# Long convolution with routed experts: three batches' experts move into the last selection, and the column loop gets more buffers

## The chip, the cores and the metric

The kernel runs on one core of one Trainium2 chip. The metric is device time in microseconds (us), the median of three runs. A core has five engines that run their own queues in order: TensorE (PE, with its weight loads shown as PEld), VectorE (DVE), ScalarE (ACT), GpSimd (POOL) and SyncE (SP), whose queue issues the plain DMAs.

## The reference

Four batches of 12608 rows with 128 channels. First a long convolution along the rows, by a Fourier transform, then a layer of experts on the 128 rows of each batch with the highest scores:

```
u = x * v
y = irfft(rfft(u, 2 * S) * rfft(h_filt, 2 * S))[:S]
x = x * y
scores = einsum('bsd,d->bs', x, w_gate)
out = x.copy()
for b in range(B):
    top_idx = argpartition(-scores[b], 128)[:128]
    xe = x[b, top_idx]
    ye = maximum(xe @ w1, 0) @ w2          # 128 -> 1024 -> 128
    out[b, top_idx] = xe + sigmoid(scores[b, top_idx])[:, None] * ye
```

`h_filt` is a small network of `pos_emb`, times a window, the same for all batches. All of it is float32.

## The kernel before

**Spectrum and tiles.** The filter's spectrum is made first (`h_hid`, `h_spec`) and kept in DRAM. Then the batches' channels go through the transform in tiles of four channels, 32 tiles a batch, 128 in all. A tile `t` passes: `stage_u` on GpSimd (two products, L215 and L216), `f_s1` on TensorE with two copies on ACT (L226, L227, L235), `dft` on TensorE (L243, copied at L246), `f_v`, `f_u`, `f_m`, `f_y` on DVE, `f_sd` on GpSimd (L420, L421; the very last tile's on DVE), and three tiles later `f_i` on TensorE, copied into `big` by ACT (L429).

**Column loop.** When a batch's 32 tiles are in `big`, `P1.run` makes the last stage, 116 columns in 29 steps of four (`hbs`), two steps to a block of eight (`blocks`, 15 of them, the last with one step). A step's matmuls (`mm`) take four matmuls for a plain column (L475) and two for a column whose sum and difference GpSimd made ahead (`comb`, L458, read at L470). `comb` makes up to four columns of each block from the third on; in batches 0 and 3 every second block gets three. `comb` has two buffers (`cm`), and is called at the end of each odd step for the block after the next. DVE multiplies a step's result with x (`fin`, L483), and `weigh` multiplies it with the gate's weights (L502), from which ACT sums each column's score (L504). The last two steps' scores are summed on DVE alone (L489). The blocks of x lie in four buffers (`xa`). Four blocks are loaded ahead, in the last tiles of the batch (`LA`). A block that is done is stored (L495), and then the load (L447) of a later block into the buffer of the block before it is issued; it waits for that store. Both stand in SP's queue.

**Selection and experts.** After the loop, the batch's 128 rows are found by a search for a threshold over the scores in 16 rounds (`TopK`, and `TopKS` with ACT doing the counts). A round counts on DVE or ACT (`counts`), adds over partitions on TensorE (`total`), and steps on DVE (`step`). Then `select` marks and numbers the rows (its last product on GpSimd is L756), `place` makes their indices (matmuls by `tots`, then L768, L772, L783), and `moe` gathers the rows (L792), loads the experts' weights (L795, L797), and computes: transpose, two halves of the first layer (L815), gate, second layer, sum (L825), scatter (L827).

**What orders it.** The selection of batches 0 to 2 runs as `Background`, a generator that is cut at `yield` marks. The tile loop calls `hook` with a letter at fixed places, and if the generator stands at that letter, its next piece is issued there: `p` behind the DFT on TensorE, `n` next to it (at least a tile after the last piece), `d` and `e` among DVE's work, `w` for GpSimd's indirect DMA, `s`, `t`, `x` for the weights and what follows. The generator of batch b goes on into the column loop of batch b + 1, where `run` calls hooks at each step and drains what is left. The last batch's selection runs alone at the end. So the experts of batches 0 and 1 lie in the column loops of batches 1 and 2, those of batch 2 in the tiles just ahead of the last loop, and those of batch 3 at the end.

The buffers share one `arena`; `OFF` gives their places. In the loops, the weights of the experts lie on `qs`, `mt` and `yz`, which the tiles use.

Of the kernel before, what the change touches and what calls it, by code (L numbers as in the profile page):

```python
# [21 lines left out]
NJ = N2 // 2 + 1  # L22
# [20 lines left out]
NE = 3  # L43
LA = range(32 - 10, 32 - 2, 2)
# [9 lines left out]
ARENA = _o  # L54
POS0, HID0 = 0, PJ * N1
# [21 lines left out]
def _tables():  # L77
# [36 lines left out]
    tk[:, 294:294 + NJ] = np.where(_valid(), 0.0, NEG)  # L114
# [23 lines left out]
def hyena_moe(ctx, tc, xg, x2, pos, bw, ww, wg, mw1, mw2, fo, c1, gx, cf, ci, wm, tk, zr, out):  # L138
# [295 lines left out]
    class P1:  # L434
        def __init__(self, b):
            self.b = b
            self.sc = small([128, NJ], f"sc_{b}", tag="sc")
            self.xa, self.s4, self.cm = {}, {}, {}
            self.mul = None
            self.nc = [NC if b in (1, 2) or k % 2 else NC - 1 for k in range(len(blocks))]  # L440

        def load_a(self, k):
            if k < len(blocks):
                j0, j1 = blocks[k]
                self.xa[k] = buf("xa", k, [128, 8, D])
# [3 lines left out]
        def comb(self, k):  # L449
# [4 lines left out]
            n = min(self.nc[k], j1 - j0)  # L454
            cm = buf("cm", k, [128, 2, NC, D])
# [22 lines left out]
        def fin(self, h):  # L478
# [3 lines left out]
            js = slice(ja % 8, ja % 8 + n)  # L482
            nc.vector.tensor_tensor(out=xa[:, js], in0=self.s4.pop(h)[:, :n], in1=xa[:, js], op=ALU.mult)  # L483
            self.weigh()
            if h < len(hbs) - 2:
# [6 lines left out]
            if ja + n == blocks[blk][1]:  # L492
# [3 lines left out]
                if blk:  # L496
                    self.load_a(blk - 1 + NX)
# [58 lines left out]
    class TopK:  # L556
        def __init__(self, b, sc, ones, f, hi, ms):
            self.b, self.sc, self.ones, self.f, self.hi, self.ms = b, sc, ones, f, hi, ms
            self.n = sc.shape[1]
# [63 lines left out]
        def rounds(self):  # L623
            for r in range(16):
# [8 lines left out]
                self.total()  # L633
                yield "d"
# [49 lines left out]
    def select(b, k, n, tr, ones, rs, ws):  # L684
# [66 lines left out]
        if b + 1 < B:  # L751
# [4 lines left out]
            nc.gpsimd.tensor_tensor(out=oh, in0=oh, in1=ws[:, :128], op=ALU.mult)  # L756
        else:
# [203 lines left out]
```

## Time and profile before

| | us |
|---|---|
| median of three runs (lowest, highest) | 978.84 (978.0, 980.4) |
| the profiled execution | 975.58 |
| its span | 973.8 |
| TensorE busy in the span | 912.4 |
| DVE, ACT, GpSimd busy | 853.9, 607.9, 763.7 |
| HBM read, written (MB) | 146.67, 41.42 |

In the profile, a line of the timeline or of a group has the line of the kernel, the engine, the operation, `out<-in` by the program's names, and the shape. Behind a bar or in square brackets stands the idle time of the engine ahead of it and what ended it. The list of waits has, behind the colon, the sum, the number and the longest of the waits. A row of windows has the stretch and its length, then for each engine its busy time and number of instructions, then the granted clock of TensorE as a share of full speed, the busy share of the DMA engines, and GB/s. A float32 matmul is recorded as two instructions. "arena" is the common buffer, so most tiles have that name; the line tells them apart.

The tiles up to the first column loop take about 160 us (from 118.8 to 278.4), then a loop and 32 tiles alternate, and the last selection begins at about 932 us.

### The profile page before, as it was taken

Reading aid. Unit: us, or ns where it says so; the run is one execution under the profiler, and the core shown is the slowest. Engines: PE = TensorE matmul, PEld = TensorE weight load, DVE = VectorE, ACT = ScalarE, POOL = GpSimd, SP = SyncE. Lnnn points to the kernel's source line nnn. Section 1 sums busy time; section 2 is a strip of 40 time slices with the busy share of each in tenths; the row PEclk is TensorE's granted clock in tenths of the full one; section 3 lists DMA queues with packets and bytes.
Section 4 is the critical chain, followed back from the end, with each engine's and each line's share of the span. In section 5 each row is a group of like instructions: output and inputs, shape, how many; then the busy total and the mean of one; then the engine's idle time right before and its main releaser. Section 6 shows DMA issues by size and latency. Waiting matters only on the chain.

```text
span 973.8 us, 37920 instructions
## 1 busy us (share of the span) xinstructions
PE 912.4 (94%) x15566; PEld 836.0 (86%) x15566; DVE 853.9 (88%) x1598; ACT 607.9 (62%) x1953; POOL 763.7 (78%) x714
## 2 busy tenths in 40 slices
PE   8999999999999999998989999989989999989925
PEld 5777789999999999997889998979989999979914
DVE  7999999999987999998977999979879999976784
ACT  6656545555558887854577878645678877545820
POOL 5898779999997499998985899988965999955700
PEclk9999999999999999999999999999999999989966
DMA  8144588667868866667688666667687666653830
GB/s 241 67 171 188 194 248 210 183 185 210 240 171 284 256 181 186 196 192 207 181 288 255 181 196 194 185 183 221 211 275 217 181 187 195 188 151 99 301 123 6
DMA packets 64960, 190.54 MB, mean 196 GB/s; under 512 B 8853, under 2 KB 15876, under 8 KB 64772
## 3 DMA queue, kind: packets, MB, share of 16 engines
q1 hardware_dynamic: 64532, 187.59, 63.4%
q8 instruction: 123, 2.02, 0.9%
q0 software_dynamic: 256, 0.52, 0.2%
q14 instruction: 49, 0.40, 0.1%
HBM read 146.67 MB, written 41.42 MB: 193 GB/s over the span
## 4 chain that ended last, share of the span: by engine, by line
PE 73%; DMA 10%; POOL 6%; DVE 5%; issue 3%; ACT 1%; SPq 1%; POOLq 0%; DVEq 0%; ACTq 0%
PE c L243 18%; PE c L226 14%; PE a L226 12%; PE a L227 7%; PE c L227 6%; DMA out_dram<-arena 5%; DMA arena<-in_x_dram 4%; PE c L379 3%; PE a L359 3%; PE c L359 3%; PE a L475 2%; POOL arena L421 2%; POOL arena L420 2%; POOL arena L215 1%; DVE ms L595 1%
## 5 line engine op out<-in xcount | busy, mean ns | idle before, releaser
L226 PE MATMUL c<-ci_sb,arena 128*56 128x116 f32 x2048 | 225.6, 263 | 0.0
L227 PE MATMUL c<-ci_sb,arena 128*55 128x116 f32 x2048 | 225.6, 263 | 0.0
L226 PE MATMUL a<-c_sb,arena 111*58 111x111 f32 x2048 | 219.9, 261 | 0.0
L227 PE MATMUL a<-c_sb,arena 111*57 111x111 f32 x2048 | 219.7, 261 | 0.0
L243 PE MATMUL c<-arena,cf_sb 128*64 128x222 f32 x2048 | 217.4, 351 | 2.2 <-DVE arena L414 1.9
L226 PEld LDWEIGHTS c<-ci_sb,arena 128*56 128x56 f32 x2048 | 208.3, 131 | 0.1
L227 PEld LDWEIGHTS c<-ci_sb,arena 128*55 128x55 f32 x2048 | 208.2, 130 | 0.0
L226 PEld LDWEIGHTS a<-c_sb,arena 111*58 111x58 f32 x2048 | 201.9, 133 | 6.6 <-issue 0.3
L420 POOL TENSOR_TENSOR arena<-arena 128x444 f32<-128x444 f32 x127 | 133.8, 1054 | 88.4 <-DVE arena L414 60.2
L227 PEld LDWEIGHTS a<-c_sb,arena 111*57 111x57 f32 x2048 | 201.8, 132 | 1.2
L235 ACT COPY arena<-a 128x444 f32<-128x444 f32 x256 | 135.6, 530 | 77.8 <-PE a L227 77.4
L243 PEld LDWEIGHTS c<-arena,cf_sb 128*64 128x64 f32 x2048 | 152.7, 137 | 28.8 <-ACT arena L235 2.3
L429 ACT COPY big<-c 128x928 f32<-128x928 f32 x128 | 118.3, 924 | 75.6 <-PE c L227 75.6
L504 ACT ACTIVATE arena<-arena 128x128 f32<-128x128 f32 x432 | 128.2, 298 | 45.2 <-DVE arena L502 44.4
L215 POOL TENSOR_TENSOR arena<-arena 111x460 f32<-111x460 f32 x128 | 150.2, 1173 | 0.0
L458 POOL TENSOR_TENSOR arena<-big 128x512 f32<-128x512 f32 (+2 forms) x104 | 119.2, 1182 | 36.4 <-PE c L470 21.4
L216 POOL TENSOR_TENSOR arena<-arena,wm_sb 111x460 f32<-111x460 f32 x128 | 139.4, 1089 | 10.0
L407 DVE TENSOR_TENSOR arena<-c,arena 128x888 f32<-128x888 f32 x128 | 138.4, 1081 | 3.8
L408 DVE TENSOR_TENSOR c<-c,arena 128x888 f32<-128x888 f32 x128 | 138.3, 1080 | 0.0
L421 POOL TENSOR_TENSOR arena<-arena 128x444 f32<-128x444 f32 x127 | 134.7, 1061 | 0.0
L246 ACT COPY arena<-c 128x444 f32<-128x444 f32 x128 | 67.8, 530 | 60.6 <-PE c L243 57.2
L475 PE MATMUL a<-big,gx_sb 128*64 128x128 f32 x1536 | 100.6, 274 | 2.4 <-DVE arena L483 1.1
(188 smaller groups left out, 1654.9 us busy)
## 6 DMA issues: line engine op xcount, KB each, us to landing
arena<-hd SPq DMA_DIRECT2D x128, 444.0 KB
arena<-in_xg_dram SPq DMA_DIRECT2D x128, 402.5 KB
arena<-in_x_dram SPq DMA_DIRECT2D x112, 224.0 KB
out_dram<-arena SPq DMA_DIRECT2D x112, 224.0 KB
hd<-arena SPq DMA_DIRECT2D x32, 444.0 KB
arena<-in_moe_w_dram SPq DMA_DIRECT2D x8, 512.0 KB
arena<-in_pos_dram SPq DMA_DIRECT2D x14, 222.0 KB
arena<-in_x_dram SPq DMA_DIRECT2D x8, 112.0 KB
```

Of the source, the lines that this page charges most:

```text
L215: nc.gpsimd.tensor_tensor(out=u[:, 0], in0=u[:, 0], in1=u[:, 1], op=ALU.mult)
L216: nc.gpsimd.tensor_tensor(out=u[:, 1].rearrange("p (s j) -> p s j", s=4), in0=u[:, 0].rearrange("p (s j) -> p s j", s=4), in1=sg, op=ALU.mult)
L226: nc.tensor.matmul(o[:h], lhsT=lhsT[:, :h], rhs=rhs, **kw)
L227: nc.tensor.matmul(o[NQ:NQ + m - h], lhsT=lhsT[:, h:], rhs=rhs, **kw)
L235: nc.scalar.copy(out=te[:, e], in_=tps[e])
L243: nc.tensor.matmul(pq[w][e * NQ:(e + 1) * NQ, c], lhsT=cf_sb[:, 2 * w + e], rhs=te[:, e, c], start=True, stop=True)
L407: nc.vector.tensor_tensor(out=mt, in0=uv, in1=ht[:, 0].unsqueeze(1).to_broadcast([128, 2, HC]), op=ALU.mult)
L408: nc.vector.tensor_tensor(out=uv, in0=uv, in1=ht[:, 1].unsqueeze(1).to_broadcast([128, 2, HC]), op=ALU.mult)
L420: eng.tensor_tensor(out=nat(sd[:, 0]), in0=nat(yz[:, 0]), in1=rev(yz[:, 1]), op=ALU.add)
L421: eng.tensor_tensor(out=nat(sd[:, 1]), in0=rev(yz[:, 0]), in1=nat(yz[:, 1]), op=ALU.subtract)
L475: nc.tensor.matmul(ps[t * NQ:(t + 1) * NQ, k], lhsT=gx_sb[:, o:o + NQ], rhs=ay[:, :, e * NJ + j], start=e == 0, stop=e == 1)
L504: nc.scalar.activation(out=wx[:, k], in_=wx[:, k], func=AF.Copy, accum_out=self.sc[:, ja + k:ja + k + 1])
```

## The change

- The experts of batches 0 to 2 no longer run in the background. Their selections end with the gather of the rows into a tile of their own, and `run` is called only after the background is drained; the loop has no hooks for it any more.
- A class `Experts` takes the three picked batches. In the last column loop it adds their gate sums on DVE (steps 4, 8, 12) and loads the weights once (steps 22 and 25). When the last selection starts, it transposes the three batches' rows, and in the rounds, behind each `total`, it issues one piece: half of a first layer, or half of a second one, or (with the next batch's first piece) the sum and the scatter. The last batch's experts are computed at the end, as before (`one`), with the same weights.
- The column loop has two more buffers for x and a third one for the sums, all three on `qs`, `mt` and `yz`. The two extra blocks are loaded, and the first three blocks' sums issued, at the beginning of `run`. All blocks have four columns of sums.
- `select` has one more `yield "n"` behind its last product on GpSimd, for batches 0 to 2.
- The last but one step's scores go the way of the others, by DVE and ACT; the mask is applied with `min` in the place of `add`.

```diff
 NE = 3
+MW = 22
...
+CE = OFF["qs"][0]
+XE = [CE + 2 * NC * D + k * 8 * D for k in range(2)]
...
-    tk[:, 294:294 + NJ] = np.where(_valid(), 0.0, NEG)
+    tk[:, 294:294 + NJ] = np.where(_valid(), -NEG, NEG)
...
-            self.nc = [NC if b in (1, 2) or k % 2 else NC - 1 for k in range(len(blocks))]
...
         def load_a(self, k):
             if k < len(blocks):
                 j0, j1 = blocks[k]
-                self.xa[k] = buf("xa", k, [128, 8, D])
+                o = k % (NX + len(XE))
+                self.xa[k] = buf("xa", o, [128, 8, D]) if o < NX else view(arena, XE[o - NX], [128, 8, D])
...
-            n = min(self.nc[k], j1 - j0)
-            cm = buf("cm", k, [128, 2, NC, D])
+            n = min(NC, j1 - j0)
+            o = (k - CB[0]) % 3
+            cm = buf("cm", o, [128, 2, NC, D]) if o < 2 else view(arena, CE, [128, 2, NC, D])
...
-                if j // 8 in CB and CO <= j % 8 < CO + self.nc[j // 8]:
+                if j // 8 in CB and CO <= j % 8 < CO + NC:
...
+            if h == len(hbs) - 1:
+                self.weigh()
             nc.vector.tensor_tensor(out=xa[:, js], in0=self.s4.pop(h)[:, :n], in1=xa[:, js], op=ALU.mult)
-            self.weigh()
-            if h < len(hbs) - 2:
+            if h < len(hbs) - 1:
+                self.weigh()
                 self.mul = xa[:, js], buf("wx", h, [128, HB, D])[:, :n], ja, n
             else:
...
                 if blk:
-                    self.load_a(blk - 1 + NX)
+                    self.load_a(blk - 1 + NX + len(XE))
...
-        def run(self, bg):
+        def run(self, ex):
             self.wg = ps2(1, [128, D], f"wg_{self.b}")
             nc.scalar.copy(out=self.wg, in_=wgb)
+            for k in range(len(XE)):
+                self.load_a(NX + k)
+            for k in range(3):
+                self.comb(CB[0] + k)
             for h in range(len(hbs)):
-                bg.now = h
-                bg.hook("p", 3)
                 self.mm(h)
                 self.fin(h)
-                if h % 2:
-                    self.comb(h // 2 + 2)
-                bg.hook("w", 2)
-                if h > 1:
-                    bg.hook("s")
-                bg.hook("t", 5)
-                bg.hook("x", 3)
-                bg.hook("n", 1)
-                for _ in range(3):
-                    bg.hook("d")
-            nc.vector.tensor_tensor(out=self.sc, in0=self.sc, in1=negm, op=ALU.add)
-            bg.drain()
+                if h % 2 and h // 2 >= CB[0]:
+                    self.comb(h // 2 + 3)
+                if ex:
+                    ex.hook(h, self.wg)
+            nc.vector.tensor_tensor(out=self.sc, in0=self.sc, in1=negm, op=ALU.min)
             return self.sc
...
                 yield "p"
                 self.total()
+                if self.ex:
+                    self.ex.step()
                 yield "d"
                 self.step(r)
...
             nc.gpsimd.tensor_tensor(out=oh, in0=oh, in1=ws[:, :128], op=ALU.mult)
+            yield "n"
...
-        ix = small([128, 1], f"ix_{b}", I32, tag=f"ix{k0}")
+        ix = small([128, 1], f"ix_{b}", I32, tag=f"ix{b}")
...
-    def moe(b, ix, ws, mb, ks):
...
+    of = out.rearrange("b p j d -> (b p j) d")
+
+    def gather(b, ix, xe):
+        nc.gpsimd.indirect_dma_start(out=xe, out_offset=None, in_=of[:(b + 1) * 2 * PR * NJ],
                                      in_offset=bass.IndirectOffsetOnAxis(ap=ix, axis=0))
...
+    def scatter(b, ix, xo):
+        nc.gpsimd.indirect_dma_start(out=of[:(b + 1) * 2 * PR * NJ],
+                                     out_offset=bass.IndirectOffsetOnAxis(ap=ix, axis=0), in_=xo, in_offset=None)
...
+    class Experts:
+        def __init__(self, picked):
+            self.picked = picked
...
+            self.m1, self.m2 = view(arena, o, [128, 1024]), view(arena, o + 1024, [128, 8, D])
+            self.hs = [view(arena, o + 2048 + 1024 * k, [128, 8, CAP]) for k in range(2)]
+            o = OFF["te"][0]
+            self.xt = view(arena, o, [128, n, CAP])
+            self.tm, self.xo = (view(arena, o + n * CAP + k * D, [128, D]) for k in range(2))
+            self.gs = small([CAP, 2 * n], "gs", tag="gs")
+            self.gen = self.work()
+
+        def hook(self, h, wg):
+            if h % 4 == 0 and 0 < h // 4 <= len(self.picked):
+                self.gate(self.picked[h // 4 - 1][2], h // 4 - 1, wg)
+            if h == MW:
+                nc.sync.dma_start(self.m1, mw1)
+            if h == MW + 3:
+                nc.sync.dma_start(self.m2, mw2.rearrange("(c p) d -> p c d", p=128))
+
+        def gate(self, xe, k, wg):
+            nc.vector.scalar_tensor_tensor(out=self.tm, in0=xe, scalar=1.0, in1=wg, op0=ALU.mult, op1=ALU.mult,
+                                           accum_out=self.gs[:, 2 * k:2 * k + 1])
+
...
+        def half(self, xt, hs, ps, f):
...
+                cc = 4 * f + c
+                mm2(hp[:, c], self.m1[:, cc * 128:(cc + 1) * 128], xt)
+            nc.scalar.activation(out=hs[:, 4 * f:4 * f + 4], in_=hp, func=AF.Relu)
+
+        def second(self, yp, hs, c0, c1):
+            for c in range(c0, c1):
+                mm2(yp, hs[:, c], self.m2[:, c], start=(c == 0), stop=(c == 7))
+
+        def finish(self, b, ix, xe, yp, k):
+            nc.vector.scalar_tensor_tensor(out=self.xo, in0=yp, scalar=self.gs[:, 2 * k + 1:2 * k + 2], in1=xe, op0=ALU.mult,
+                                           op1=ALU.add)
+            scatter(b, ix, self.xo)
+
+        def start(self):
+            tp = ps1(2, [128, 512], "xeT")
+            for k, (b, ix, xe) in enumerate(self.picked):
+                nc.tensor.transpose(tp[:, k * CAP:(k + 1) * CAP], xe, ident)
+            nc.scalar.copy(out=self.xt, in_=tp[:, :len(self.picked) * CAP].rearrange("p (k c) -> p k c", c=CAP))
+            self.step()
+
+        def step(self):
+            next(self.gen, None)
+
+        def work(self):
+            last = None
+            for k, (b, ix, xe) in enumerate(self.picked):
+                hs = self.hs[k % 2]
+                self.half(self.xt[:, k], hs, 0, 0)
+                if last:
+                    self.finish(*last)
+                yield
+                self.half(self.xt[:, k], hs, 1, 1)
+                if k == 0:
+                    for i in range(len(self.picked)):
+                        self.sigmoid(i)
+                yield
+                yp = ps1(2, [128, 512], f"my_{b}")[:, :D]
+                self.second(yp, hs, 0, 4)
+                yield
+                self.second(yp, hs, 4, 8)
+                last = b, ix, xe, yp, k
+                yield
+            self.finish(*last)
+            yield
+
+        def one(self, b, ix, xe):
+            tp = ps1(0, [128, 512], f"xeTp_{b}")
+            nc.tensor.transpose(tp[:, :CAP], xe, ident)
+            xt = self.xt[:, 0]
+            nc.scalar.copy(out=xt, in_=tp[:, :CAP])
+            hs = self.hs[0]
+            for f in range(2):
+                self.half(xt, hs, f, f)
+            self.gate(xe, 0, wgb)
+            self.sigmoid(0)
+            yp = ps1(3, [128, 512], f"my_{b}")[:, :D]
+            self.second(yp, hs, 0, 8)
+            self.finish(b, ix, xe, yp, 0)
...
+    picked = []
+
+    def topk_one(b, sc, ex):
...
         k = (TopKS if b + 1 < B else TopK)(b, sc, onesb, f, hi, ms)
+        k.ex = ex
+        if ex:
+            ex.start()
         yield from k.rounds()
         yield "n"
...
-        yield from moe(b, ix, ws, mb, ((3, 3), (3, 3), (0, 1), (3, 2))[b])
+        xe = small([128, D], f"xe_{b}", tag=f"xe{b}") if b + 1 < B else ws[:, 128:256]
+        yield "w"
+        gather(b, ix, xe)
+        if ex:
+            warm(NWARM)
+            ex.one(b, ix, xe)
+        else:
+            picked.append((b, ix, xe))
...
-            if t >= NT - 3:
-                bg.hook("s")
-                bg.hook("t")
...
-            bg.hook("x")
...
-            bg.at = 0
-            sc = ph.pop(b).run(bg)
-            bg = Background(topk_one(b, sc))
+            bg.drain()
+            ex = Experts(picked) if b + 1 == B else None
+            sc = ph.pop(b).run(ex)
+            bg = Background(topk_one(b, sc, ex))
```

More of the change, by code (lines that the diff above doesn't have):

```diff
@@ L558, in __init__ @@
             self.b, self.sc, self.ones, self.f, self.hi, self.ms = b, sc, ones, f, hi, ms
+            self.ex = None
             self.n = sc.shape[1]
@@ L784, in place @@
         return ix
-    def moe(b, ix, ws, mb, ks):
-        xe, xt, tm = (ws[:, 128 * k:128 * k + 128] for k in range(3))
-        xo = ws[:, 384:512]
-        m1, m2, hs = mb
-        of = out.rearrange("b p j d -> (b p j) d")[:(b + 1) * 2 * PR * NJ]
-        yield "w"
-        nc.gpsimd.indirect_dma_start(out=xe, out_offset=None, in_=of,
-                                     in_offset=bass.IndirectOffsetOnAxis(ap=ix, axis=0))
-        yield "s"
-        nc.sync.dma_start(m1, mw1)
-        yield "t"
-        nc.sync.dma_start(m2, mw2.rearrange("(c p) d -> p c d", p=128))
-        yield "x"
-        if b + 1 == B:
-            warm(NWARM)
-        yield "p"
-        tp = ps1(ks[0], [128, 512], f"xeTp_{b}")
-        nc.tensor.transpose(tp[:, :CAP], xe, ident)
-        yield "d"
-        nc.scalar.copy(out=xt, in_=tp[:, :CAP])
-        gs = small([CAP, 2], f"gs_{b}", tag="gs")
-        wg = ps2(1, [128, D], f"wgm_{b}") if b + 2 < B else wgb
-        for hf in range(2):
-            yield "p"
-            hp = ps1(ks[hf], [128, 4, CAP], f"mh_{b}_{hf}")
-            for c in range(4):
-                cc = 4 * hf + c
-                mm2(hp[:, c], m1[:, cc * 128:(cc + 1) * 128], xt)
-            yield "d"
-            nc.scalar.activation(out=hs[:, 4 * hf:4 * hf + 4], in_=hp, func=AF.Relu)
-        yield "d"
-        nc.vector.scalar_tensor_tensor(out=tm, in0=xe, scalar=1.0, in1=wg, op0=ALU.mult, op1=ALU.mult,
-                                       accum_out=gs[:, 0:1])
-        nc.scalar.activation(out=gs[:, 1:2], in_=gs[:, 0:1], func=AF.Sigmoid)
-        yield "p"
-        yp = ps1(ks[0], [128, 512], f"my_{b}")
-        for c in range(8):
-            mm2(yp[:, :D], hs[:, c], m2[:, c], start=(c == 0), stop=(c == 7))
-        yield "d"
-        nc.vector.scalar_tensor_tensor(out=xo, in0=yp[:, :D], scalar=gs[:, 1:2], in1=xe, op0=ALU.mult, op1=ALU.add)
-        yield "w"
-        nc.gpsimd.indirect_dma_start(out=of, out_offset=bass.IndirectOffsetOnAxis(ap=ix, axis=0), in_=xo,
-                                     in_offset=None)
@@ L830, in topk_one @@
-    def topk_one(b, sc):
+    of = out.rearrange("b p j d -> (b p j) d")
+    def gather(b, ix, xe):
+        nc.gpsimd.indirect_dma_start(out=xe, out_offset=None, in_=of[:(b + 1) * 2 * PR * NJ],
+                                     in_offset=bass.IndirectOffsetOnAxis(ap=ix, axis=0))
+    def scatter(b, ix, xo):
+        nc.gpsimd.indirect_dma_start(out=of[:(b + 1) * 2 * PR * NJ],
+                                     out_offset=bass.IndirectOffsetOnAxis(ap=ix, axis=0), in_=xo, in_offset=None)
@@ L836, in topk_one @@
         ws = buf("ws", 0, [128, 640])
-        q0, u0 = OFF["qs"][0], OFF["u"][0]
-        mo = (u0 + 3 * 2 * XC, OFF["cm"][0], u0) if b + 2 == B else (q0, q0 + 1024, q0 + 2048)
-        mb = [view(arena, o, s) for o, s in zip(mo, ([128, 1024], [128, 8, D], [128, 8, CAP]))]
         rk, oh = yield from select(b, k, NJ, tri, onesb, rst, ws)
         ix = yield from place(b, rk, oh, jio, NJ, 3, ws[:, :128])
-        yield from moe(b, ix, ws, mb, ((3, 3), (3, 3), (0, 1), (3, 2))[b])
+        xe = small([128, D], f"xe_{b}", tag=f"xe{b}") if b + 1 < B else ws[:, 128:256]
[6 more added lines that the diff above has]
+            picked.append((b, ix, xe))
     for t in bank2[2:] + bank1 + bank2[:2]:
```

4 lines of the change are left out of this document (added).

## The prediction

> **What bounds the kernel now.** I read the page first, then the list of waits, then the chain of waits and the timeline around its irregular places, and last the windows.
>
> ```profile
> span 973.8 us, 37920 instructions
> PEclk9999999999999999999999999999999999989966
> PE 73%; DMA 10%; POOL 6%; DVE 5%; issue 3%; ACT 1%; SPq 1%; POOLq 0%; DVEq 0%; ACTq 0%
> ```
>
> The chain lies on TensorE for 73%, and the clock is full until the last two slices, the last selection. So three kinds of time can be won: TensorE work, holes in TensorE's queue, and the selection at the end. The list of waits names a hole and a transfer:
>
> ```profile
> PEld a L226 <- POOL arena L756: 10.4, 3, 3.5
> DVE arena L483 <- DMA arena<-in_x_dram: 21.1, 24, 2.5
> ```
>
> The first is three waits, one for each of the first three selections. The timeline shows what each costs, by the starts of the forward DFT (L243), one a tile:
>
> ```profile
> 455.28 0.54 PE L243 MATMUL c<-arena,cf_sb 128*64 128x222 f32 x4
> 459.89 0.54 PE L243 MATMUL c<-arena,cf_sb 128*64 128x222 f32 x4
> 442.48 0.41 PE L243 MATMUL c<-arena,cf_sb 128*64 128x222 f32 x2
> 446.76 0.46 POOL L756 TENSOR_TENSOR arena<-arena 128x128 f32<-128x128 f32 x1
> 450.67 0.54 PE L243 MATMUL c<-arena,cf_sb 128*64 128x222 f32 x4
> 646.06 0.41 PE L243 MATMUL c<-arena,cf_sb 128*64 128x222 f32 x2
> 655.90 0.54 PE L243 MATMUL c<-arena,cf_sb 128*64 128x222 f32 x4
> 851.65 0.41 PE L243 MATMUL c<-arena,cf_sb 128*64 128x222 f32 x2
> 862.75 0.35 PE L243 MATMUL c<-arena,cf_sb 128*64 128x222 f32 x2
> 857.00:860.00 3.00, 3.00 (x38) 3.00 (x36) 0.00 (x0) 0.53 (x1) 2.92 (x4) 0.50 0.00 0
> ```
>
> A plain tile takes 4.61 us (455.28 to 459.89). The tiles with the wait take 8.19, 9.84 and 11.10, and no later tile is shorter to make up for it. The last row is a window behind the third wait: its clock column reads 0.50, so that wait also left TensorE at half clock.
>
> **The change, part by part.** All of it against the profiled execution, 975.58 us for a span of 973.8.
>
> *The selection step.* `select` ends with a GpSimd product (L756) and `place` begins with matmuls that read it. They are issued at the head of the next tile, while GpSimd still has two products of `stage_u` ahead of L756; all of TensorE's tile queues behind them. The added step lets one tile pass. L756 ends at 447.22 (446.76 + 0.46); without the wait the next DFT starts at 442.48 + 4.61 = 447.09, and the matmuls follow that DFT, later than L756's end. So the waits go: (8.19 − 4.61) + (9.84 − 4.61) + (11.10 − 4.61) = 15.3 us. Next late is the gather, one tile later:
>
> ```profile
> 459.33 1.13 POOL L792 DMA_INDIRECT arena<-out_dram,ix  x1 [0.17 <-DVE arena L414]
> ```
>
> The first stands 17 us ahead of its loop (476.85, below), so a tile is covered. If that cover were gone, the drain ahead of the loop would pay, a tile at most (4.6).
>
> *The column loops.* Their first and last matmuls:
>
> ```profile
> 278.44 0.33 PE L475 MATMUL a<-big,gx_sb 128*64 128x128 f32 x2
> 322.77 0.61 PE L470 MATMUL a<-arena,gx_sb 128*64 128x128 f32 x8
> 476.85 3.71 PE L475 MATMUL a<-big,gx_sb 128*64 128x128 f32 x64
> 526.40 0.61 PE L470 MATMUL a<-arena,gx_sb 128*64 128x128 f32 x8
> 682.09 0.33 PE L475 MATMUL a<-big,gx_sb 128*64 128x128 f32 x2
> 732.00 0.61 PE L470 MATMUL a<-arena,gx_sb 128*64 128x128 f32 x8
> 884.54 0.33 PE L475 MATMUL a<-big,gx_sb 128*64 128x128 f32 x2 [1.03 <-ACT big L429]
> 927.23 0.61 PE L470 MATMUL a<-arena,gx_sb 128*64 128x128 f32 x8
> ```
>
> That is 44.9, 50.2, 50.5 and 43.3 us, together 188.9. The second and third carry an expert each:
>
> ```profile
> 504.28 0.32 PE L226 MATMUL c<-arena 128*64 128x128 f32 x1 [1.71 <-ACT arena L805]
> 510.26 0.32 PE L226 MATMUL c<-arena 128*64 128x128 f32 x1 [0.96 <-ACT arena L815]
> 515.87 0.32 PE L226 MATMUL c<-arena 128*64 128x128 f32 x1 [0.59 <-ACT arena L815]
> 517.67 0.39 PE L475 MATMUL a<-big,gx_sb 128*64 128x128 f32 x4
> ```
>
> Its second layer takes 1.8 us (515.87 to 517.67), the first has as many matmuls, the transpose is small: about 4 us of work and 3.3 of waits. Taking it out leaves 50.2 − 7.3 = 42.9. What TensorE alone needs comes from the steps:
>
> ```profile
> 486.78 0.33 PE L470 MATMUL a<-arena,gx_sb 128*64 128x128 f32 x2 [0.80 <-POOL arena L458]
> 520.29 0.28 PE L475 MATMUL a<-big,gx_sb 128*64 128x128 f32 x2
> ```
>
> From 517.67 to 520.29 are two steps: one with two summed columns takes 1.31 us. One of the four without takes 1.86 (64 matmul records, two steps, in 3.71): 4 × 1.86 + 25 × 1.31 = 40.2. GpSimd's first sums still come after its last tile, so the 0.8 above and a little before it stay, 1.2 as I estimate: 41.4. The first and last loop summed three columns instead of four in every second block; the change gives them the same 40.2, for a fourth column more of GpSimd time, which the third buffer and the earlier start cover.
>
> Now the transfers. A block is, by the code, 2 × 56 × 8 × 128 × 4 bytes in and as much out; two more buffers give two blocks of lead, but each load still waits for an output two places ahead of it in SP's queue.
>
> ```profile
> 483.21 1.06 POOL L421 TENSOR_TENSOR arena<-arena 128x444 f32<-128x444 f32 x1
> 485.25 0.79 SPq L495 DMA_DIRECT2D out_dram<-arena  x2
> 297.60 4.19 DMA out_dram<-arena
> 701.69 7.12 DMA out_dram<-arena
> 301.85 4.90 DMA arena<-in_x_dram
> 500.00:504.00 4.00, 2.48 (x42) 1.99 (x38) 2.48 (x4) 2.40 (x17) 3.59 (x4) 1.00 0.91 339
> ```
>
> The new buffers lie on `yz`, which GpSimd reads until 484.27, 7.4 us into the loop; the two new loads stand at SP's head until then, and the first outputs queue behind them. They leave at about 9, land at 14 and free the seventh block's load. From there two blocks take one output (4.2) and two issues of about 0.8, so 2.9 us a block; the 14th block lands at 14 + 7 × 2.9 + 4.9 = 39 us, about when TensorE is two steps from the end. So TensorE and transfers are nearly level. I take 42.5 for the first three loops (between 41.4 and 44.9, nearer the first as no load is waited for early), and 41.2 for the last, where GpSimd is free sooner and DVE has three gate sums to add. Sum 168.7, so −20.2 us.
>
> At 1.31 us a step the loop moves 918 KB in 2.62 us, 350 GB/s, above the 339 of the fullest window. The Trainium skill ("DMA: Bandwidth & Descriptors", Specifications) gives about 358 GB/s as the limit of one core's HBM traffic, by which the 41.4 could just be held; the window shows less.
>
> *The tiles ahead of the last loop.* There the third expert filled holes of TensorE. Without it the loop may start up to a microsecond earlier (the 1.03 in front of its first matmul), or 3.4 later if a hole of 3 us halves the clock as above. I take 0.
>
> *The last selection.* Sixteen rounds, with twelve pieces of 8 matmuls between them:
>
> ```profile
> 953.04 0.16 PE L226 MATMUL c<-st,onesb 128*64 128x3 bf16 x1 [1.16 <-DVE ms L595]
> 954.42 0.16 PE L226 MATMUL c<-st,onesb 128*64 128x3 bf16 x1 [1.16 <-DVE ms L595]
> 948.00:952.00 4.00, 0.65 (x6) 0.40 (x6) 3.41 (x27) 0.00 (x0) 0.00 (x0) 0.50 0.01 2
> L825 DVE SCALAR_TENSOR_TENSOR arena<-c,gs,arena 128x128 f32<-128x128 f32 x3 | 1.0, 346 | 4.4 <-PE c L227 4.4
> ```
>
> A round takes 1.38 us and leaves TensorE idle for 1.16. What waits behind a piece is the next round's total, on TensorE; behind an expert's result, the round's threshold, on DVE. A piece is half of a layer, 0.9 at full clock: hidden. At 0.50 it is 1.8, and each round grows by some 0.7. The row of 948 shows half clock, but with TensorE nearly idle; the pieces fill it. I take two slow rounds, 1.5, until the clock is up, and three results of 0.35 on DVE, partly inside its wait for TensorE: 0.7. Sum +2.2 (0.7 to 9.1). The three scatters run on an idle GpSimd, the weights load once, during the loop's last steps. The Trainium skill ("TensorE: Matmul & The Clock Gate", Part 1) has the clock go full after a busy window of about 3.4 us and half after an idle one; by that the slow rounds are two or three, as taken, and the rounds of the row of 948 agree with the idle half of it.
>
> The mask (`min` for `add`) and the reordered last weighing change no count on the path: 0.
>
> Sum: −15.3 − 20.2 + 0 + 2.2 = −33.3, so 942.3 us in a profiled execution. The median of the runs (978.84) is 3.3 above the profiled one, so 945.6.
>
> **The rivals.**
> 1. *The loops stay at the transfers' pace.* The first and last keep 44.9 and 43.3, the other two fall to 44.9: −10.9 instead of −20.2. For it: the 21.1 us of waits for inputs. Against: two blocks of lead. 954.9. Chance 0.13.
> 2. *The wait for L756 only moves* with its step, or the chain falls on another GpSimd result: 945.6 + 15.3 = 960.9. For it: GpSimd is busy 2.92 of 3 us in the row of 857. Against: the end at 447.22. This is also the case that the step does not do what it says. Chance 0.07.
> 3. *The pieces never lift the clock*: 12 × 0.7 = 8.4 instead of 1.5: 952.5. Chance 0.07.
> 4. *Slower: SP's queue chokes.* With both new loads at its head and more in flight, an output takes 7.1 us, as at 701.69, where weights shared the queue. A block then takes (7.1 + 1.6) / 2 = 4.35; a loop 14 + 8 × 4.35 + 4.9 + 1.3 = 55, the last some 51: 216, +27 for −20: 945.6 + 47 = 993. It beats the other gains once outputs take over about 6.2 us throughout (loops of 50.5). Against: the weights leave those loops. Chance 0.03.
>
> The forecast keeps 0.70. Faster by over 0.3% (about what a measurement here tells from no change) 0.95, within 0.02 (rivals 1 to 3 together with outputs of 6 us), slower 0.03.
>
> **Range.** Low: loops at 41.4 and 40.2 (−4.3), rounds at 0.7 (−1.5), −1 ahead of the last loop: 939. High: rival 1 with part of rival 3, and rival 3: 957. Rivals 2 and 4 lie outside, and about a tenth for sizes that are off.
>
> **What would show it.** No wait for L756 on TensorE, no tile over 6 us; loops of 41 to 43 us with waits for inputs under 2 us each; rounds of 1.4 us but for the first ones, clock 1.00 in the middle rounds. It is wrong if a GpSimd wait stands in the tile after, if L483 still waits 5 us or more a loop, or if the rounds stay near 2.1.

## The result and the profile after

The changed kernel takes 943.56 us (median of 6 runs, 941.11 to 948.21) against 978.66 for the kernel before in the same session (6 runs, 975.87 to 980.4): a ratio of 0.965, 95% interval 0.962 to 0.967. The forecast was 945.6 (939 to 957). The profiled execution took 944.23 us for a span of 942.3.

The head of the page, with the clock of the 40 slices and the chain of waits by engine:

```profile
span 942.3 us, 37826 instructions
PEclk9999999999999999999999999999999999999998
PE 79%; DVE 6%; POOL 5%; DMA 4%; ACT 3%; issue 3%; SPq 0%; POOLq 0%; ACTq 0%; DVEq 0%
```

The chain's share on TensorE rose from 73% to 79%, that of DMA fell from 10% to 4%: transfers were what gave way. The clock's digits now read 9, which stands for 90% or more, up to the last slice, through most of the rounds too.

The timeline around the step that follows the first selection (TensorE's forward DFT, now L246, once a tile, and the last GpSimd product, now L760):

```profile
442.33 1.72 PE L246 MATMUL c<-arena,cf_sb 128*64 128x222 f32 x16
446.97 1.70 PE L246 MATMUL c<-arena,cf_sb 128*64 128x222 f32 x16
451.81 0.54 PE L246 MATMUL c<-arena,cf_sb 128*64 128x222 f32 x3
446.64 0.46 POOL L760 TENSOR_TENSOR arena<-arena 128x128 f32<-128x128 f32 x1
```

The product ends at 447.10, the DFT starts at 446.97, and the matmuls that read the product come behind that DFT: as forecast to about a tenth of a microsecond. The tile takes 4.84 (446.97 to 451.81), where before there were 8.19, 9.84 and 11.10. The list of waits no longer has L760 ahead of TensorE.

The four column loops by windows (the stretch and its length; then busy time of PE, PEld, DVE, ACT, POOL with instructions; granted clock, DMA share, GB/s), and the wait of `fin` (now L489) for its inputs over the whole span:

```profile
279.20:322.50 43.30, 41.28 (x735) 40.03 (x734) 37.24 (x60) 31.98 (x201) 40.46 (x35) 1.00 0.71 232
473.40:516.90 43.50, 41.00 (x734) 40.06 (x734) 37.72 (x60) 32.05 (x201) 40.76 (x36) 1.00 0.72 233
667.40:709.40 42.00, 40.78 (x734) 40.07 (x734) 37.83 (x60) 32.31 (x202) 40.72 (x35) 1.00 0.71 237
854.60:894.60 40.00, 39.96 (x729) 39.80 (x730) 35.22 (x61) 32.95 (x208) 31.49 (x26) 1.00 0.71 230
```

```profile
DVE arena L489 <- DMA arena<-in_x_dram: 7.9, 10, 1.8
```

TensorE is busy for 39.96 of the 40.0 us of the last loop: there it is the bound. The waits for inputs fell from 21.1 us to 7.9 and lie, but for 0.3, in the first three loops (2.6, 3.0, 2.0).

Stage by stage, in microseconds of the profiled executions. A loop goes from its first matmul to the end of its last; "behind" is from there to the next loop's first matmul; the last selection goes from the last loop's end to the end of the span.

| kernel | loops | their sum | behind loops 1, 2, 3 | last selection | span |
|---|---|---|---|---|---|
| before | 44.9, 50.2, 50.5, 43.3 | 188.9 | 153.5, 155.1, 151.9 | 45.9 | 973.8 |
| after | 43.3, 43.5, 42.0, 40.0 | 168.8 | 150.9, 150.5, 145.2 | 47.7 | 942.3 |
| n_only | 44.1, 50.9, 50.2, 44.9 | 190.0 | 150.8, 151.1, 146.5 | 46.1 | 963.6 |
| no_n | 42.0, 42.3, 42.5, 40.0 | 166.7 | 155.3, 155.5, 151.5 | 46.6 | 954.3 |
| old_no_experts | 44.0, 44.6, 44.7, 44.6 | 178.0 | 155.5, 153.5, 151.3 | 46.3 | 964.7 |
| four_x | 45.9, 45.6, 44.8, 43.6 | 179.8 | 151.6, 150.6, 146.0 | 48.7 | 955.7 |
| late_loads | 42.0, 42.2, 42.0, 40.0 | 166.2 | 150.1, 150.1, 144.9 | 47.5 | 936.7 |

From before to after, the span fell by 31.5: loops −20.1, the three stretches −13.9, the last selection +1.8, and +0.8 ahead of the first tile, which the change does not touch.

### The profile page after: what moved, and what is told of

Read it like the earlier page. It is cut to its first block, busy times and chain, and to the rows that moved or that the text cites. A ratio compares the mean times of both kernels' runs of the same rounds, so it can differ in the third digit from the quotient of the medians.

```text
span 942.3 us, 37826 instructions
## 1 busy us (share of the span) xinstructions
PE 902.8 (96%) x15518; PEld 831.1 (88%) x15518; DVE 854.4 (91%) x1570; ACT 613.3 (65%) x1983; POOL 769.3 (82%) x714
## 4 chain that ended last, share of the span: by engine, by line
PE 79%; DVE 6%; POOL 5%; DMA 4%; ACT 3%; issue 3%; SPq 0%; POOLq 0%; ACTq 0%; DVEq 0%
PE c L246 18%; PE c L230 10%; PE c L229 10%; PE a L230 10%; PE a L229 9%; PE a L479 5%; PE c L382 3%; PE a L362 3%; PE c L362 3%; PE c L479 3%; PE a L474 2%; ACT arena L510 2%; DMA out_dram<-arena 1%; POOL arena L423 1%; POOL arena L424 1%
## 5 line engine op out<-in xcount | busy, mean ns | idle before, releaser
L229 PE MATMUL c<-ci_sb,arena 128*56 128x116 f32 x2048 | 224.8, 263 | 4.3 <-POOL arena L423 2.0
L246 PE MATMUL c<-arena,cf_sb 128*64 128x222 f32 x2048 | 217.6, 351 | 2.2 <-DVE arena L417 1.9
L229 PE MATMUL a<-c_sb,arena 111*58 111x111 f32 x2048 | 217.0, 259 | 0.0
L230 PE MATMUL a<-c_sb,arena 111*57 111x111 f32 x2048 | 216.8, 259 | 0.0
L229 PEld LDWEIGHTS c<-ci_sb,arena 128*56 128x56 f32 x2048 | 206.5, 130 | 5.9 <-POOL arena L423 2.2
L229 PEld LDWEIGHTS a<-c_sb,arena 111*58 111x58 f32 x2048 | 199.2, 132 | 4.3 <-issue 0.3
L230 PEld LDWEIGHTS a<-c_sb,arena 111*57 111x57 f32 x2048 | 199.0, 131 | 2.9
L246 PEld LDWEIGHTS c<-arena,cf_sb 128*64 128x64 f32 x2048 | 154.1, 137 | 27.6 <-ACT arena L238 2.3
L510 ACT ACTIVATE arena<-arena 128x128 f32<-128x128 f32 x448 | 133.0, 298 | 27.4 <-DVE arena L508 25.2
L462 POOL TENSOR_TENSOR arena<-big 128x512 f32<-128x512 f32 (+1 forms) x104 | 125.1, 1262 | 8.9 <-ACT big L432 5.6
```

The lines of the kernel that those rows point to most:

```text
L229: nc.tensor.matmul(o[:h], lhsT=lhsT[:, :h], rhs=rhs, **kw)
L230: nc.tensor.matmul(o[NQ:NQ + m - h], lhsT=lhsT[:, h:], rhs=rhs, **kw)
L246: nc.tensor.matmul(pq[w][e * NQ:(e + 1) * NQ, c], lhsT=cf_sb[:, 2 * w + e], rhs=te[:, e, c], start=True, stop=True)
L510: nc.scalar.activation(out=wx[:, k], in_=wx[:, k], func=AF.Copy, accum_out=self.sc[:, ja + k:ja + k + 1])
```

## The experiments

**n_only** and **no_n**: the later step alone, and everything but the step.

```
             nc.gpsimd.tensor_tensor(out=oh, in0=oh, in1=ws[:, :128], op=ALU.mult)
+            yield "n"        # n_only: added to the kernel before
-            yield "n"        # no_n: taken from the changed kernel
```

> The kernel before with the one added yield behind the last GpSimd product of select, and nothing else. Theory (the three TensorE waits for L756 are lost whole, and one tile is enough to hide them): the three long tiles of 8.2, 9.8 and 11.1 us fall to about 4.8, 14.6 us less: 964.0 from 978.7. Rival (the wait only moves to another GpSimd result or is paid in the drain): within 3 us of 978.7, and a tile over 7 us stays.

Measured: 965.27 (962.77 to 966.59), ratio 0.986 (0.982 to 0.991), against 976.14 for before then.

> The changed kernel without the added yield, all else kept. Theory (the step's gain does not hang on the other parts): three tiles of 8 to 11 us come back, +14.6: 958.2 from 943.6. Rival (with the experts gone from the background, GpSimd would be on time anyway): +5 at most.

Measured: 958.1 (955.4 to 962.44), ratio 0.981 (0.975 to 0.986). Without the step the wait is back on TensorE in the changed kernel:

```profile
PE a L229 <- POOL arena L760: 9.2, 3, 3.1
```

Its three tiles take 9.85 each instead of 4.84, +15.0 together, and its time is 14.5 above the changed kernel's. In n_only the three tiles fell by 14.6, but the span only by 10.2 and the time by 10.9: other stages of that one execution were longer by 4.4 (the loops alone by 1.1, the stretches less their tiles by 2.6; one later tile took 5.58). So the step takes about 15 us out of TensorE's tiles in either kernel. That no part of it comes back later is shown with the other parts of the change; for n_only, where the 4.4 come from stays open.

**old_no_experts**: the kernel before without the experts' layers of the first three batches (the rows are selected and gathered, nothing more; their weights are not loaded either), to see what the experts alone cost the loops.

```
-        yield from moe(b, ix, ws, mb, ((3, 3), (3, 3), (0, 1), (3, 2))[b])
+        if b + 1 < B:
+            yield "w"
+            nc.gpsimd.indirect_dma_start(out=ws[:, :128], ...)
+            return
+        yield from moe(b, ix, ws, mb, ((3, 3), (3, 3), (0, 1), (3, 2))[b])
```

> The kernel before with the experts of batches 0 to 2 left out (their rows are gathered and go no further, so out lacks their sums); buffers, sums and steps as before. Theory (the experts cost the loops their matmuls and their waits): the second and third loop fall from 50.2 and 50.5 to about 43, the last tiles by 0.8: 963.3 from 978.7, so -15.4. Rival (the transfers bind at the first loop's pace): both fall to 44.9 only, -11.6: 967.

Measured: 965.75 (963.46 to 966.49), ratio 0.986 (0.982 to 0.991). The second and third loop take 44.6 and 44.7, not 43, and the waits for inputs are as long as before:

```profile
DVE arena L483 <- DMA arena<-in_x_dram: 21.2, 29, 1.9
```

The rival was right: with four buffers, the loops fall only to the pace of the transfers.

**four_x**: the changed kernel without the two new input blocks.

```
-XE = [CE + 2 * NC * D + k * 8 * D for k in range(2)]
+XE = []
```

> The changed kernel with four input blocks instead of six (no extra loads at the head of run), three sums buffers and all else kept. Theory (two blocks of lead keep inputs ahead of TensorE): waits of L483's line for inputs rise from 8 to over 20 us, loops go to 44 to 45.5 us from 43.3, 43.5, 42.0 and 40.0: +6 to +10, 951.5. Rival (the experts' going alone made the loops short): +1 or less.

Measured: 956.26 (955.06 to 957.62), ratio 0.977 (0.973 to 0.981) against 0.965: some 12 us above the changed kernel. The waits are back:

```profile
DVE arena L489 <- DMA arena<-in_x_dram: 24.3, 23, 1.9
```

The four loops sum to 179.8 instead of 168.8. So the loops' 20.1 divide into 9.1 for all the rest (the experts above all) and 11.0 for the two blocks. Executions with six blocks scatter by some 2 us here: the sum is 166.7 in no_n and 169.2 in weights_early (below).

**two_sums**: the changed kernel with two sums buffers, as before.

```
-            o = (k - CB[0]) % 3
+            o = k % 2
...
-            for k in range(3):
+            for k in range(2):
...
-                    self.comb(h // 2 + 3)
+                    self.comb(h // 2 + 2)
```

> The changed kernel with two sums buffers instead of three and the sums issued two blocks ahead, all else kept. Theory (GpSimd at 2.5 us a block and TensorE at 2.62 are so close that two buffers lock them to each other): GpSimd waits for TensorE at each block, loops 0.5 to 1.5 us longer each: +2 to +5, 947. Rival (the third buffer does nothing, as GpSimd is never behind): within 1 us of 943.6.

Measured: 944.47 (942.09 to 946.65), ratio 0.965 (0.962 to 0.967), the loops at 167.3. The third sums buffer does nothing that can be measured.

**three_cols**: the changed kernel with the number of summed columns of before.

```
+            self.nc = [NC if b in (1, 2) or k % 2 else NC - 1 for k in range(len(blocks))]
...
-            n = min(NC, j1 - j0)
+            n = min(self.nc[k], j1 - j0)
...
-                if j // 8 in CB and CO <= j % 8 < CO + NC:
+                if j // 8 in CB and CO <= j % 8 < CO + self.nc[j // 8]:
```

> The changed kernel with the summed columns of before: three instead of four in every second block of the first and the last loop. My theory: a column that is not summed costs TensorE (1.86 - 1.31) / 2 = 0.28 us, six or seven of them 1.7 to 1.9; the last loop, at TensorE's pace, grows by that from 39.96, the first, which waits for inputs, by less than 1: +2, about 946. The rival, that both loops have slack: last loop 40.0 to 40.5, total as the changed kernel.

Measured: 943.28 (942.89 to 945.7), ratio 0.966 (0.963 to 0.968). The last loop takes 41.3 instead of 40.0, less than the 1.7 expected but the right direction; the first takes 42.8, no longer than in the changed kernel. In the whole time 1.3 us is not to be told from the scatter.

**no_pieces**: the changed kernel without the experts' layers of the first three batches (selected and gathered rows stay as they are).

```
-                if self.ex:
-                    self.ex.step()
...
-        if ex:
-            ex.start()
```

> The changed kernel with the experts of batches 0 to 2 left out (gathered, never computed nor scattered); weights and gate sums stay. Theory (in the rounds the pieces cost one cold piece ahead of the first total, 1.3 us, and the late second weight matrix, 1.5, and nothing else): rounds of 1.38 throughout, 2.8 us less: 940.8. Rival (pieces also cost each round through TensorE or DVE): 5 us less or more. Rival (the clock that the pieces keep up pays for them): the same 943.6.

Measured: 943.72 (941.83 to 944.82), ratio 0.965 (0.962 to 0.967). The last selection took 44.9 instead of 47.7, but other stages of this execution were longer, so the time shows nothing of it. The same code of the last selection took 45.4 to 49.7 in six executions (below), so three experts cost the rounds some 3 us and no more can be said; that the clock which the pieces hold up pays for them is not seen, since from the last step to the end both take about 18.1. In the kernel before, taking the experts out shortened the loops by 10.9 (188.9 to 178.0).

**weights_early** and **early**: where the last selection lost its 1.8. The first issues the experts' weights at steps 12 and 15 of the last loop instead of 22 and 25. The second also transposes the rows at step 20 and puts two pieces ahead of the rounds.

```
-MW = 22
+MW = 12
...
+            if h == MW + 8:          # early
+                self.turn()          # the transposes and their copy
...
+            self.step()              # early: a second piece ahead of the rounds
```

> The changed kernel with the weights issued at steps 12 and 15 of the last loop instead of 22 and 25. Theory (the 2.8 us round waits for the second matrix, which was issued at 897.8 behind outputs in SP's queue): that round falls to 1.4, 1.5 us less: 942.1. Rival (the weights then delay the loop's inputs): that round falls, but the last loop grows by as much: the same 943.6.

Measured: 946.13 (944.72 to 950.78), ratio 0.968 (0.966 to 0.971). The round of 2.8 us is gone, the longest take 1.81 and 1.79 at half clock; but the first step comes 8.5 us after the loop instead of 6.4, and why stays open.

> As weights_early, and the picked rows are transposed in the loop (step 20) and two pieces instead of one issued ahead of the first round. Theory (TensorE goes cold between the loop's end and the first piece, because the transposed rows are copied only behind ACT's last scores): pieces at full clock from the loop's end, the first total no later than DVE asks for it: 1.3 us less than weights_early, 940.8. Rival (the hole between the two pieces and the first total, about 2 to 3 us, makes it cold again): as weights_early, 942.1.

Measured: 945.77 (943.31 to 951.34), ratio 0.968 (0.965 to 0.970). In early all rounds without the search's half-way step take 1.35 to 1.39; the first steps (L617), from the timeline:

```profile
902.32 0.16 DVE L617 SCALAR_TENSOR_TENSOR st<-c,tk_sb 128x3 f32<-128x3 f32 x1
903.68 0.16 DVE L617 SCALAR_TENSOR_TENSOR st<-c,tk_sb 128x3 f32<-128x3 f32 x1 [0.15 <-PE c L230]
905.07 0.15 DVE L617 SCALAR_TENSOR_TENSOR st<-c,tk_sb 128x3 f32<-128x3 f32 x1
```

But the last loop then waits 2.1 us for its inputs (weights_early: 4.0) and takes 40.6 (40.1). Both were expected to be faster than the changed kernel, and neither time shows it.

**best**: both matrices, the transposes and their copy at step 20, right behind the last input load, and two pieces ahead of the rounds as in early.

```
-MW = 22
+MW = 20
...
-            if h == MW + 3:
                 nc.sync.dma_start(self.m2, mw2.rearrange("(c p) d -> p c d", p=128))
+                self.turn()
```

> The changed kernel with both weight matrices issued at step 20 of the last loop, right behind the last load of an input block, the rows of the three batches transposed there too, and two pieces of the experts ahead of the rounds. Theory: the late second matrix and the cold first piece were the 2.8 us by which the end of the last selection is longer than without pieces, and behind the last input load the weights delay no input: rounds all 1.36 to 1.39, last loop 40.0 to 40.3, no input wait over 1 us in it, total 941 to 942. The rival: the weights, ahead of the last outputs, hold back something else (the gather of the last selection, the first pieces), and the total is 943 to 946.

Measured: 942.36 (941.25 to 945.76), ratio 0.965 (0.962 to 0.968). The last selection took 45.0, with no input wait in the last loop, but that loop took 40.6, and the first round still took 1.88, at half clock. Kernels whose last selection has the code of the changed one show 45.4 (three_cols), 47.5 (late_loads) and 49.7 (two_sums), so neither 45.0 nor the time proves a gain.

**in_loop**: the pieces in steps 13 to 28 of the last loop instead of the rounds, the weights at steps 2 and 5. The pieces' results also go to other buffers in PSUM, the memory into which this kernel's matmuls write.

```
-MW = 22
+MW = 2
...
+            if h == 13:
+                self.start()
+            if h > 13:
+                self.step()
...
-                if self.ex:
-                    self.ex.step()
```

> The changed kernel with the twelve pieces of the first three batches' experts at steps 13 to 28 of the last column loop instead of the rounds of the last selection (weights loaded at steps 2 and 5). My theory, that time on TensorE in the last loop counts in full while in the rounds it is hidden: the loop ran at TensorE's pace (39.96 us), so it grows by 12 pieces of 0.93, about 11; the rounds go back to 1.38 each and the end of the selection gets 2.8 shorter: about +8, 951 to 953. The rival, that the loop has slack because transfers bind it: last loop +0 to +3, total 941 to 944.

Measured: 969.81 (968.21 to 975.01), ratio 0.993 (0.991 to 0.996). Neither expectation held: the last loop takes 66.2, 26.3 more. The list of waits inside it:

```profile
DVE arena L489 <- PE a L474: 15.0, 9, 2.6
POOL arena L462 <- PE a L474: 12.4, 3, 5.3
PE c L229 <- DVE arena L508: 8.7, 6, 1.5
PE c L229 <- ACT arena L850: 2.7, 1, 2.7
PE c L229 <- ACT arena L835: 2.0, 2, 1.0
```

TensorE's matmuls of the pieces (L229) waited 13.4 us: for the weighing (L508), for the copy of the transposed rows (L850) and for the relu (L835). All the matmuls of the next step stood behind them. With the work of 12 pieces of about 0.93 that is 25 of the 26. The 8.7 may come from where this kernel put the second layers' results, in the PSUM buffer of the gate weights that L508 reads; this was not told apart. The 11 of pure TensorE time stand without it.

**late_loads**: the two new loads behind the first block's outputs instead of at the head of the loop.

```
-            for k in range(len(XE)):
-                self.load_a(NX + k)
...
-                if blk:
-                    self.load_a(blk - 1 + NX + len(XE))
+                for k in (range(NX, NX + len(XE)) if blk == 0 else [blk - 1 + NX + len(XE)]):
+                    self.load_a(k)
```

> The changed kernel with the loads of the two additional input blocks issued behind the first block's outputs in each loop, instead of at the loop's head, where they wait for GpSimd and the outputs queue behind them. Theory: what delays the loops' transfers is that wait at the head of SP's queue (the first outputs left at 6 us into the second loop), so the outputs leave some 4 us sooner and the input waits of 2.0 to 3.0 in each of the first three loops go: loops 1 and 2 come to 41 to 42, total 938 to 941. The rival, that the sum of the bytes binds: the loops stay at 42 to 43.5, total 942 to 945; the loop may also get longer, if the two blocks arrive too late for steps 8 and 10.

Measured: 938.87 (938.56 to 941.32), ratio 0.961 (0.958 to 0.964), the fastest of all: 3.5 and 4.4 under best and three_cols, which ran on the same chip at 941.25 to 945.76. SP's issues in the second loop, first of the changed kernel (loop from 473.40), then of late_loads (from 470.12):

```profile
481.00 1.84 SPq L450 DMA_DIRECT2D arena<-in_x_dram  x4
482.94 3.11 SPq L501 DMA_DIRECT2D out_dram<-arena  x4
488.56 1.00 SPq L450 DMA_DIRECT2D arena<-in_x_dram  x2
```

```profile
476.13 0.77 SPq L501 DMA_DIRECT2D out_dram<-arena  x2
477.75 1.67 SPq L450 DMA_DIRECT2D arena<-in_x_dram  x4
479.52 0.76 SPq L501 DMA_DIRECT2D out_dram<-arena  x2
```

In the changed kernel nothing leaves for 7.6 us: the loads wait for DVE and then for GpSimd to be done with the buffers, and the outputs of two blocks stand behind them until 482.94, 9.5 into the loop. In late_loads the first output leaves at 6.0 (the expectation took these 6 for the changed kernel's), and the loads still find their buffers free at 7.6. All input waits of the first three loops go, and what is left in the whole span lies in the last one:

```profile
DVE arena L489 <- DMA arena<-in_x_dram: 2.0, 2, 1.6
```

The loops by windows:

```profile
278.00:320.10 42.10, 40.90 (x740) 40.16 (x738) 39.66 (x63) 33.92 (x211) 40.51 (x35) 1.00 0.77 256
470.10:512.30 42.20, 40.81 (x737) 40.09 (x736) 39.61 (x62) 33.88 (x210) 40.85 (x36) 1.00 0.75 256
662.40:704.40 42.00, 40.79 (x736) 40.09 (x736) 39.56 (x62) 33.82 (x210) 40.77 (x35) 1.00 0.75 250
849.30:889.30 40.00, 39.98 (x729) 39.78 (x730) 33.68 (x59) 31.89 (x201) 31.53 (x26) 1.00 0.74 245
```

The first three loops move 250 to 256 GB/s instead of 232 to 237: more of a loop's bytes move inside it (10.8 MB in the first instead of 10.0), fewer behind it. DVE is also level with TensorE at a loop's end: the first tile behind each of the first three loops takes a plain tile's time (under 4.75), where the changed kernel shows 5.41, 4.98 and 4.94. The two belong together. In no_n the loops are nearly as short with the loads at the head (42.0, 42.3, 42.5), but the tiles behind them take 5.09, 5.08 and 5.75. So the loops alone do not show the gain; the way from the first loop's start to the last one's does: 571.3 us in late_loads, 575.3 to 576.9 in the eight traces with the loads at the head and otherwise the changed kernel's tiles, 574.2 in no_n less its 15.0. Of the 5.6 between the spans of the changed kernel and late_loads, 1.2 lie ahead of the first tile, which the edit does not touch. Late_loads and best were not put together.

## Why the prediction was right, point by point

*Select step: −15.3 forecast, −14.6 in the trace.* The reason held: the end of the product, the start of the DFT and the order behind it came as worked out, no later tile of the changed kernel lost it again, and n_only and no_n show it with and without the rest. Each tile keeps 0.2 over a plain one. Why equal waits had cost 8.19, 9.84 and 11.10 was the clock behind them: full, half for 3.4 us, and half for 6.8.

```profile
447.00:451.00 4.00, 3.72 (x76) 3.68 (x78) 1.07 (x5) 1.18 (x3) 3.92 (x5) 1.00 0.91 232
651.00:655.00 4.00, 4.00 (x54) 4.00 (x56) 0.00 (x0) 0.95 (x2) 3.92 (x4) 0.59 0.72 189
```

*Loops: −20.2 forecast, −20.1 measured, the sum right, the way to it only partly.* "Taking it out leaves 50.2 − 7.3 = 42.9" fails as a step of its own: with the experts out and four buffers, the loops take 44.6 and 44.7 (old_no_experts), the transfers' pace of rival 1, which it put at 44.9. The two blocks took away that floor, in all four loops, and that is worth 11.0 (four_x). The forecast reached the same sum because it set the loops by the transfers with six buffers afterwards: outputs that leave at about 9 (measured 9.5) and 42.5 a loop (43.3, 43.5, 42.0). The estimate of 1.2 for the wait for the first sums fits the first three loops: in late_loads, where no transfer holds them, it is TensorE's only wait (1.2, 1.4, 1.2) and they take 42.0 to 42.2. The last loop was put at 41.2 and came out at TensorE's 40.0: that wait and the three gate sums cost it nothing. The fourth summed column is worth 1.3 there (three_cols), and the third sums buffer, named as the cover for the fourth column, covers nothing (two_sums).

*Input waits "under 2 us each": 2.6, 3.0 and 2.0 in the first three loops.* The forecast saw why, the loads at SP's head, but counted it as given. late_loads shows that it was a price, 4.1 us from the first loop's start to the last one's: in these two traces 2.6 of the loops and 1.5 of the tiles behind them, where DVE was late. The forecast had no term for those tiles.

*Tiles ahead of the last loop: 0 forecast, −0.8 measured*, from the start of the last DFT to the loop (12.56 before, 11.79 after). The feared half clock stayed out of this execution by luck. TensorE had holes of 1.97, 0.60, 0.84 and 1.03 us there and kept 1.00 (first row); in two_sums, with the same tiles and holes of 1.98, 0.59 and 1.04, it ran at 0.50 for 3.4 us (second row) and took 12.29:

```profile
850.00:854.00 4.00, 2.74 (x48) 2.07 (x42) 1.91 (x4) 1.28 (x2) 0.00 (x0) 1.00 0.52 132
849.80:853.10 3.30, 3.30 (x36) 2.83 (x34) 2.16 (x4) 0.93 (x1) 0.00 (x0) 0.50 0.35 94
```

Of the eleven kernels whose last tiles carry no expert, eight have such a stretch there and take 11.80 to 12.57; the changed kernel, best and late_loads have none and take 11.79. So the forecast of 0 was the better number, and a half clock costs up to 0.8 here, not the 3.4 that was feared.

*Last selection: +2.2 forecast, +1.8 measured, close by luck and from other causes in part.* Six executions with the changed kernel's code there take 45.4 to 49.7 (mean 47.6; their first step comes 4.8 to 8.2 us behind the loop), three with the code of before 45.9 to 46.3: about +1.5 on average. The forecast counted two rounds at half clock and three results on DVE. The timeline and windows of the changed kernel's first rounds:

```profile
893.79 0.36 SPq L817 DMA_DIRECT2D arena<-in_moe_w_dram  x1
897.20 0.46 ACT L848 COPY arena<-c 128x384 f32<-128x384 f32 x1
897.76 0.64 SPq L819 DMA_DIRECT2D arena<-in_moe_w_dram  x1
898.95 0.45 PE L229 MATMUL a<-arena 128*64 128x128 f32 x1 [3.87 <-DVE ms L600]
901.00 0.16 DVE L617 SCALAR_TENSOR_TENSOR st<-c,tk_sb 128x3 f32<-128x3 f32 x1 [1.49 <-PE c L230]
905.29 0.16 DVE L617 SCALAR_TENSOR_TENSOR st<-c,tk_sb 128x3 f32<-128x3 f32 x1 [1.61 <-PE c L230]
906.41 0.34 DVE L840 SCALAR_TENSOR_TENSOR arena<-c,gs,xe 128x128 f32<-128x128 f32 x1
906.67 0.15 DVE L617 SCALAR_TENSOR_TENSOR st<-c,tk_sb 128x3 f32<-128x3 f32 x1
```

```profile
900.00:904.00 4.00, 2.39 (x30) 2.23 (x26) 2.35 (x18) 1.47 (x5) 0.00 (x0) 0.76 0.86 287
904.00:908.00 4.00, 3.36 (x58) 3.00 (x60) 2.51 (x19) 0.43 (x1) 0.96 (x1) 1.00 0.10 36
916.00:920.00 4.00, 2.35 (x38) 1.81 (x35) 3.64 (x28) 0.28 (x2) 0.93 (x1) 1.00 0.01 2
924.00:928.00 4.00, 3.13 (x20) 2.70 (x20) 3.25 (x17) 0.00 (x0) 0.00 (x0) 0.50 0.00 0
```

The first piece runs cold, as forecast: it starts at 898.95, after 3.87 us of idle TensorE, and the first step waits 1.49 for it. The one long round, 2.83, ends at 905.29 for another reason, the second weight matrix (L819), which left only at 897.76, behind outputs in SP's queue. The list of waits for 896 to 926 has it:

```profile
PE c L229 <- DMA arena<-in_moe_w_dram: 1.8, 1, 1.8
```

A DVE result fits between two steps (906.41 in a round of 1.38) and costs nothing. The clock reads 1.00 from 904 until the pieces end, so rival 3 (pieces that never lift it) is out. The two slow rounds of the forecast do come in other executions: in three_cols rounds of 1.75 and 1.78, 0.4 longer each instead of 0.7, lie in this stretch:

```profile
901.00:904.00 3.00, 3.00 (x34) 3.00 (x32) 2.23 (x18) 0.87 (x4) 0.00 (x0) 0.50 0.53 202
```

early removes the cold piece and the late matrix, best all but one round of 1.88, with no gain that the time shows.

*The offset of 3.3 between profile and median.* It did not carry over: the profiled execution after is 0.7 above its median. The sum alone put the profiled execution at 942.3, and it took 944.23; in the profiles the gain is 31.4 instead of 33.3, from the 1.5 of the tiles behind the loops, the 0.7 of the select step and the 0.8 ahead of the first tile, less the 0.8 won ahead of the last loop and the 0.4 at the end. The forecast of the median came within 2.0 because these errors partly cancel: the gain was 1.9 too large, the offset 4.0.

*The rivals.* 1 describes the change without the two blocks, not the change. 2 fell with L760 gone from TensorE's waits. 4 named the place where the two loads do harm, SP's head, but its outputs of 7.1 us did not come: the loops stayed under 44.

## What to carry to other kernels

When one cost is taken out of a stage, work out which limit it falls to next, and price the next part from there: here the experts alone gave 5 to 6 us in each of two loops, and the blocks behind them as much again over all four. A load that waits for a buffer does not only come late, it holds everything behind it in its queue; let what is ready leave first. Work that is free beside a chain of small dependent steps (the rounds) can cost more than its own length in a stage that its engine bounds.

## What the runs showed of the chip

TensorE needs little to keep its clock: at 916 to 920 it is busy 2.35 of 4 us and has 1.00. The same rounds without pieces, at 948 of the kernel before, are busy 0.65 of 4 and have 0.50, and once the pieces end the clock falls back to 0.50 (924 to 928). How long a hole it stands is no fixed number here: of the three waits for L756 before, idle times of 3.08, 3.09 and 3.07, the first left it at 1.00 and the others at 0.50, and holes of up to 2 us ahead of the last loop left it at 1.00 in three kernels and brought 0.50 in eight. The half-clock stretches in these traces last 3.4 us or a multiple of it. The Trainium skill ("TensorE: Matmul & The Clock Gate", Part 1) has the clock go full after a busy window of about 3.4 us and half after an idle one; the length of the stretches agrees, and the runs add that being busy three fifths of the time kept the clock full here, and a sixth of the time did not raise it.

Mixed loads and stores are not held to the 232 to 237 GB/s that the first three loops of the changed kernel show: late_loads moves 250 to 256 over the same loops by order alone. The order closes gaps and does not raise the peak: the fullest 12 us have 314 GB/s in late_loads, 310 in the changed kernel and 307 before. The fullest 12 and 4 us of late_loads:

```profile
307.00:319.00 12.00, 12.00 (x224) 12.00 (x222) 11.77 (x19) 11.75 (x74) 11.85 (x11) 1.00 0.90 314
860.30:864.30 4.00, 4.00 (x78) 4.00 (x76) 3.95 (x7) 3.82 (x26) 3.88 (x4) 1.00 0.88 347
```

The Trainium skill ("DMA: Bandwidth & Descriptors", Specifications) gives about 358 GB/s as the limit of one core's HBM traffic; no 4 us of these loops reached it, so the order in the queue was the first thing to look at, not that limit.
